# Attention with a top-8 MLP: candidates of fifteen token tiles picked early, the last tile run through the MLP whole

## The chip, the cores and the metric

One core of one Trainium2 chip runs the program. The metric is the device time of one execution in microseconds (us); several runs of a kernel are compared by their median.

## What is computed

The input is 2048 tokens of 448 values in bf16. Attention comes first: layer norm, 16 query heads of 28 values, one key and one value head for all of them, softmax, the output projection, and the residual sum h. Then comes an MLP for eight tokens only:

```python
x = layernorm(h)                         # 2048 x 448
r = x @ w_r                              # one score per token
idx = argsort(-r)[:8]
g = silu(x[idx] @ w_gate); u = x[idx] @ w_up      # 448 -> 1792
y = ((g * u) @ w_down) * sigmoid(r[idx])          # 1792 -> 448
out = h + x, and on the eight rows idx + y
```

So 2040 output rows are h + x, and eight rows get an addend. Which eight is known only when all 2048 scores are.

## The kernel before

Tokens are in 16 tiles of 128 (`NT`), which are also the 16 query blocks (`NB`). The attention loop runs over the blocks. In each, TensorE (PE) makes score tiles in groups of two or three PSUM banks, ScalarE (ACT) takes their exponential (L719), VectorE (DVE) makes a share of the exponentials by integer arithmetic (L744, L753, with GpSimd, POOL, in L755), and PE multiplies by V into the accumulator bank. A group is a unit of the loop; a block has 17. Units 2, 5 and 11 of a block (`TWO`) are two banks wide and not three, and the bank that is left over serves the odd jobs of other blocks (`misc`).

When a block's accumulator is complete, `close_acc` (L763) copies it to `Ot` and `post_block` (L599) divides by the softmax sum. It sends the sums through DRAM (`scr`) into a spread layout `Lc`, takes a reciprocal (L603), sends that back to DRAM, reads it broadcast over partitions into `Rb` (256 KB), and POOL multiplies (L609) into `On`: four DMAs on the queue of SyncE (SP), one after the other. `out_proj` (L612) is the projection of a block: four matmuls, the residual sum into `hbuf` (L617), the layer norm's statistics, `outf` = h + x (L644; L637 for the last tile), `xn` = x (L647; L640), and the tile's scores `r_col` (L650, L653). Blocks up to 13 have their `out_proj` two blocks later in the loop; block 14's is at the end of the last block, and block 15's behind the loop.

The tail comes behind the last `out_proj`, from L859 on. It checks that the softmax sums lie in a safe range and writes `flag`; every engine reads `flag` at its end, and an exact second program runs if it isn't zero. Then: the 2048 scores in one row by a DMA, the eight largest and their places (L885, L886), sums of bf16 parts that carry the indices through PE, one-hot matrices `oh` and `ohT`, 64 matmuls that gather the eight rows of x (L916), gate and up (56 matmuls each, eight columns wide), silu by exp and reciprocal, down (14 matmuls), and then for all 16 tiles a matmul with `ohT` that spreads the eight results over 128 rows, a sum with `outf` on ACT (L949) or DVE (L952), and four output DMAs of four tiles each.

Who runs what in which order is planned when the program is built: each operation is given to a graph with an engine, a duration, a priority and what it reads and writes; the planner (`plan`, L146) simulates the engines with these durations and fixes one order for each engine, which then runs it in order with semaphore waits. A lower priority number goes first. `G.prio` is mostly the time in the loop (64 units a block). DMAs all go through SP's order; the planner lets one land 2.7 us after its issue. Line L422 is the helper of every matmul, L425 of every transpose, L439 of every DMA.

Of the kernel before, what the change touches and what calls it, by code (L numbers as in the profile page):

```python
# [8 lines left out]
ALU = mybir.AluOpType  # L9
# [309 lines left out]
def _main(nc, G, sb, ps, psb, flag, scr, A_x, A_wq, A_wk, A_wv, A_wo, B_w_r, B_w_gate, B_w_up, B_w_down, out,  # L319
# [59 lines left out]
    ofin = xnT[:, :, :].rearrange("p a b -> p (a b)")[:, 0:NT * D].rearrange("p (t d) -> p t d", d=D)  # L379
# [113 lines left out]
    for i in range(4):  # L493
# [105 lines left out]
    def post_block(b):  # L599
# [56 lines left out]

    NVB = [0] + [4] * (NB - 1)
    LEAD = 4
    TWO = (2, 5, 11)
    LAG = 4  # L660
    slots = []
    for b in range(NB):
# [148 lines left out]
    else:  # L811
# [22 lines left out]
        for b in range(NB):  # L834
            at(64.0 * b + 64.0 + (LAG + 1.2) * m0, close_acc, b)
# [211 lines left out]
```

## Time and profile before

| | us |
|---|---|
| median of 3 runs (458.55 to 459.06) | 458.83 |
| the profiled execution's own time | 457.83 |
| its span, first to last instruction | 455.6 |
| last accumulator copy of the loop (L764) starts | 397.47 |
| last `out_proj` starts | 409.53 |
| eight largest scores: search starts | 417.28 |
| gather of eight rows starts | 425.04 |
| output stage starts | 441.78 |

The profile gives each instruction with its start from the beginning of the span, its length, the engine and the line. PE is the matmuls, PEld the weight loads. A bracket behind a row is the idle time of that engine before it and what ended it. PEclk is the granted clock of PE as a share of 2.4 GHz: 1.00 is the upper level, 0.50 the lower, 1.2 GHz. The loop takes 23.03 us a block.

### The profile page before, as it was taken

How to read it: one execution, taken by the hardware profiler on the slowest of the kernel's cores; microseconds unless marked ns; L12 is line 12 of the kernel's file. 1: busy time of each engine (PE TensorE's matmuls, PEld its weight loads, DVE VectorE, ACT ScalarE, POOL GpSimd, SP SyncE). 2: the span in 40 equal slices, each digit the busy share in tenths (PEclk: the TensorE clock that was granted, in tenths of full speed). 3: DMA queues.
4: the chain of work that ended last, by engine and by line, in shares of the span. 5: the costliest groups of instructions: out<-in, count | busy, mean ns of one | idle time of the engine just before them, and what ended most of it. 6: DMA issues, size and time to landing. Idle time of an engine off the chain costs nothing.

```text
span 455.6 us, 8732 instructions
## 1 busy us (share of the span) xinstructions
PE 335.5 (74%) x3583; PEld 121.5 (27%) x3583; DVE 343.5 (75%) x696; ACT 370.3 (81%) x309; POOL 188.6 (41%) x198
## 2 busy tenths in 40 slices
PE   3898787878787878787777777778787777601685
PEld 2454222212222323222222222222222122100630
DVE  6875668889797979797979797878787878626333
ACT  3778889999999999999999999898989898801012
POOL 3242134543636363636363636363636453740000
PEclk9999999999999999999999999999999999955565
DMA  7971000000000000000000000000000000000005
GB/s 211 230 205 28 2 12 15 9 19 27 1 27 0 22 6 24 3 24 4 22 7 17 10 16 12 11 15 12 16 10 19 4 23 6 23 25 1 1 1 167
DMA packets 15973, 14.68 MB, mean 32 GB/s; under 512 B 5992, under 2 KB 12920, under 8 KB 15928
## 3 DMA queue, kind: packets, MB, share of 16 engines
q1 hardware_dynamic: 15928, 14.05, 11.0%
q8 instruction: 31, 0.51, 0.5%
q14 instruction: 14, 0.11, 0.1%
HBM read 11.94 MB, written 2.10 MB: 31 GB/s over the span
## 4 chain that ended last, share of the span: by engine, by line
DVE 49%; PE 32%; ACT 10%; issue 5%; POOL 1%; DMA 1%; POOLq 0%; SPq 0%
PE ps L422 30%; DVE Y L744 24%; ACT P L719 10%; DVE Y L753 8%; DVE bn L619 2%; DVE junk L650 2%; DVE Q L527 2%; DVE Ot L764 2%; DVE hbuf L617 2%; DVE r_col L653 2%; PE ps L425 1%; DVE xnT L572 1%; DVE K L582 1%; DMA wq_sb<-in_A_wq_dram 1%; DVE idx L886 1%
## 5 line engine op out<-in xcount | busy, mean ns | idle before, releaser
L719 ACT ACTIVATE P<-ps 128x1536 bf16<-128x1536 f32 (+2 forms) x281 | 358.3, 1401 | 29.1 <-PE ps L422 26.7
L744 DVE TENSOR_SCALAR Y<-ps 128x512 int16<-128x512 f32 x240 | 165.3, 689 | 58.6 <-PE ps L422 58.5
L755 POOL TENSOR_TENSOR Y<-Y,step 128x1024 int32<-128x1024 int32 x60 | 113.5, 1892 | 151.3 <-DVE Y L753 89.7
L422 PE MATMUL ps<-Q,K 32*128 32x512 bf16 x1024 | 112.9, 388 | 61.1 <-DVE Y L744 45.6
L422 PE MATMUL ps<-Y,Vs 128*32 128x512 bf16 x960 | 88.2, 388 | 17.7 <-DVE Ot L764 11.3
L753 DVE TENSOR_SCALAR Y<-Y 128x2048 int16<-128x2048 int16 x120 | 82.6, 688 | 0.1
L422 PE MATMUL ps<-P,Vs 128*32 128x512 bf16 x784 | 75.7, 389 | 0.5 <-ACT P L719 0.5
L422 PEld LDWEIGHTS ps<-Q,K 32*128 32x128 bf16 x1024 | 33.3, 91 | 159.0 <-ACT P L719 126.3
L422 PEld LDWEIGHTS ps<-Y,Vs 128*32 128x32 bf16 x960 | 22.5, 94 | 60.9 <-issue 19.7
L422 PE MATMUL ps<-zero 128*32 128x512 bf16 x107 | 32.8, 386 | 0.0
L422 PEld LDWEIGHTS ps<-P,Vs 128*32 128x32 bf16 x784 | 19.0, 93 | 33.1 <-issue 29.9
L644 POOL TENSOR_SCALAR x_sb<-hbuf,st 128x448 bf16<-128x448 f32 x15 | 14.8, 984 | 31.4 <-DVE st L633 31.4
L609 POOL TENSOR_TENSOR On<-Ot,Rb 128x256 bf16<-128x256 f32 x32 | 23.4, 751 | 7.3 <-DMA Rb<-l_scr 7.3
L422 PE MATMUL ps<-xnT,wq_pad 112*128 112x128 bf16 x256 | 20.6, 229 | 0.6 <-DVE mv L540 0.6
L422 PE MATMUL ps<-wo_pad,On 128*128 128x448 bf16 x64 | 15.8, 369 | 6.5 <-POOL On L609 6.5
L595 POOL TENSOR_SCALAR Vs<-Vf 128x64 bf16<-128x64 f32 (+1 forms) x36 | 9.0, 249 | 22.7 <-DVE Vf L592 21.0
L617 DVE TENSOR_TENSOR hbuf<-ps,x_sb 128x448 f32<-128x448 f32 x16 | 9.9, 617 | 10.1 <-PE ps L422 10.1
L422 PEld LDWEIGHTS ps<-xnT,wq_pad 112*128 112x128 bf16 x256 | 15.5, 102 | 7.2 <-issue 7.1
L949 ACT ACTIVATE xnT<-ps 128x448 bf16<-128x448 f32 x8 | 4.4, 544 | 12.8 <-PE ps L422 12.8
L527 DVE TENSOR_SCALAR Q<-ps,qone 128x512 bf16<-128x512 f32 x16 | 11.9, 744 | 1.9 <-PE ps L422 1.9
L624 ACT ACTIVATE st<-st 128x1 f32<-128x1 f32 x1 | 0.2, 202 | 16.0 <-DVE st L621 16.0
L422 PEld LDWEIGHTS ps<-zero 128*32 128x32 bf16 x107 | 10.2, 97 | 7.0 <-issue 1.0
(124 smaller groups left out, 221.1 us busy)
## 6 DMA issues: line engine op xcount, KB each, us to landing
Rb<-l_scr SPq DMA_DIRECT2D x16, 256.0 KB
out_dram<-xnT SPq DMA_DIRECT2D x4, 448.0 KB, 3.4
wg_sb<-in_B_w_gate_dram SPq DMA_DIRECT2D x1, 1568.0 KB, 15.3
wu_sb<-in_B_w_up_dram SPq DMA_DIRECT2D x1, 1568.0 KB, 22.4
wd_sb<-in_B_w_down_dram SPq DMA_DIRECT2D x1, 1568.0 KB, 25.5
x_sb<-in_A_x_dram SPq DMA_DIRECT2D x3, 448.0 KB, 5.9
wq_sb<-in_A_wq_dram SPq DMA_DIRECT2D x2, 196.0 KB, 3.2
wo_pad<-in_A_wo_dram SPq DMA_DIRECT2D x4, 98.0 KB
```

What stands on the lines that cost most here:

```text
L422: return lambda e: e.matmul(o, lhsT=l, rhs=r, start=start, stop=stop)
L527: G.op(DV, lambda e: e.tensor_scalar(Q[:, q, :, :].rearrange("p g n -> p (g n)"), ps[:, bank, :], qone[:, 0:1], None, ALU.add), dvt(512), ...
L609: G.op(PO, lambda e, c=c: e.tensor_tensor(On[:, rb, c], Ot[:, rb, c], Rb[:, rb, c], ALU.mult), 750, reads=[("Ot", rb), ("Rb", rb)], writes ...
L617: G.op(DV, lambda e: e.tensor_tensor(hbuf[:, hr, :], ps[:, bank, 0:D], x_sb[:, t, :], ALU.add), dvt(D), reads=[pk(bank), ("x", t)], writes ...
L619: G.op(DV, lambda e: e.bn_stats(bn6[:, t, :], hbuf[:, hr, :]), dvt(D), reads=[("h", hr)], writes=[("bn6", t)])
L644: G.op(PO, lambda e: e.tensor_scalar(outf[:, t, :], hbuf[:, hr, :], st[:, t, 5:6], st[:, t, 6:7], ALU.mult, ALU.add), 800, reads=[("h", hr ...
L650: G.op(DV, lambda e: e.scalar_tensor_tensor(junk[:, :], hbuf[:, hr, :], st[:, t, 4:5], w_rb[:, :], ALU.mult, ALU.mult, accum_out=st[:, t, ...
L653: G.op(DV, lambda e: e.scalar_tensor_tensor(r_col[:, t:t + 1], st[:, t, 6:7], sw[:, 0:1], st[:, t, 2:3], ALU.mult, ALU.add), 80, reads=[(" ...
L719: G.op(AC, lambda e: e.activation(P[:, s0:s0 + w, :], ps[:, b0:b0 + w, :], ACT.Exp, bias=-(ZERO + SHIFT) * OCT, scale=OCT), w * 427 + 50, ...
L744: G.op(DV, lambda e: e.tensor_scalar(Y[:, y, 0, q, :].bitcast(I16), ps[:, VB, :], 0.0, 32639.0 - STEP[3], ALU.max, ALU.min), dvt(512), rea ...
L753: done = [G.op(DV, lambda e, c=c: e.tensor_single_scalar(y[c].bitcast(I16), y[0].bitcast(I16), STEP[c], ALU.add), 600, reads=r, writes=[(" ...
L755: G.op(PO, lambda e: e.tensor_tensor(y[3].bitcast(I32), y[0].bitcast(I32), step3[:, 0:1].broadcast_to([128, 1024]), ALU.add), 2050, reads= ...
```

## The change

The softmax division of blocks 14 and 15 no longer waits for DRAM: a matmul with a constant 0/1 matrix `selb` (fp32) spreads the sums over partitions in PSUM, ACT makes 1/L as exp(-ln L), and for block 15 DVE multiplies instead of POOL. (The sums still go to DRAM and into `Lc` for the check.) `out_proj` of block 14 moves from the end of the loop to unit 11 of the last block; in that block units 2, 7 and 11 are the narrow ones. Output tiles 0 to 14 are written as soon as `outf` is there, one DMA each, 112 KB.

A new `stage1` takes the eight best of tiles 0 to 14: the scores as 15 rows, `max` and `max_index` in each row, two small DMAs that put the 120 candidate scores in one row and their indices in one column, `max` and `max_index` over 120, fp32 matmuls that carry values and indices to columns and rows, the one-hot `oh`, 60 gather matmuls, 15 matmuls that gather the eight rows of `outf` (`os8`), gate, up, silu (ACT's own function) and down for these eight.

The last tile's 128 tokens all go through the MLP: transpose, gate and up with 128 columns (56 matmuls each, N = 128), silu, down (14 matmuls, N = 448). Whether a token is among the best eight is decided by counts: how many scores of its tile and how many of the candidates beat it (DVE, `wst`); the result is a factor of 0 or sigmoid(r). The candidates are tested in the same way against the last tile. Tile 15 is written with one DMA, and the eight candidate rows by an indirect DMA that POOL issues, behind all the other output DMAs. ACT loads the table with silu once, behind its last exp. The planner gets a priority of -3000 for the last tile's work; `stage1` has about 1015 to 1020, `out_proj` of block 15 1044.

The diff, cut to its core:

```diff
     def post_block(b, bank=None):
...
+        if b < NB - 2:
             G.op(DV, lambda e: e.reciprocal(Rc[:, rb, :], Lc[:, b, :]), 150, reads=[("Lc", b)], ...
             dma(scr[b, 1]..., Rc[:, rb, :], [("scr1", b)], reads=[("Rc", rb)])
             dma(Rb[:, rb, :], scr[b, 1]..., reads=[("scr1", b)]).lat = 3900.0
+        else:
+            G.op(PE, mm(ps[:, bank, :], selb[:, :], Ot[:, rb, :], True, True), 900, mode="F",
+                 reads=["selb", ("Ot", rb)], writes=[pk(bank)], prio=G.prio - 40)
+            G.op(AC, lambda e: e.activation(Rb[:, rb, :], ps[:, bank, :], ACT.Ln), 480, ..., prio=G.prio - 300)
+            G.op(AC, lambda e: e.activation(Rb[:, rb, :], Rb[:, rb, :], ACT.Exp, scale=-1.0), 520, ..., prio=G.prio - 300)
...
+                G.op(DV, lambda e, c=c: e.tensor_tensor(On[:, rb, c], Ot[:, rb, c], Rb[:, rb, c], ALU.mult), 335, ...
     def out_proj(b, bank):
...
+        if not tail:
+            evs.append(dma(out_v[:, t, :], outf[:, t, :], [("out", t)], reads=[("outf", t)], prio=G.prio + 30))
+    def stage1():
+        q = G.prio
+        G.op(DV, ... rp <- r_col ...); G.op(PE, ... rp x ident -> VB ...); G.op(DV, ... r16 ...)
+        G.op(DV, lambda e: e.max(c8[:, :], r16[:, :]), 200, ...)
+        dma(crow[0:1, :].rearrange("o (t k) -> o t k", k=8), c8[:, :], ["crow"], reads=["c8"])
+        G.op(DV, lambda e: e.max_index(i8[:, :], c8[:, :], r16[:, :]), 260, ...)
...
+        dma(cidx[:, :], i8f[:, :], ["cidx"], reads=["i8f"])
+        G.op(DV, lambda e: e.max(top8[:, :], crow[:, :]), 190, ...)
+        G.op(DV, lambda e: e.max_index(pos8[:, :], top8[:, :], crow[:, :]), 260, ...)
...
+        G.prio = q + 6
+        pieces([mm(psg[0:CK, ch, :], xn[:, t, ch * CK:(ch + 1) * CK], oh[:, t, :], t == 0, t == NT1 - 1)
+                for ch in range(NCH) for t in range(NT1)], 10, 35, ..., writes=[pk(VB)])
+        pieces([mm(ps[0:8, VB, 0:D], oh[:, t, :], outf[:, t, :], t == 0, t == NT1 - 1) for t in range(NT1)], 3, 189, ...
+        G.op(DV, lambda e: e.tensor_copy(os8, ps[0:8, VB, 0:D]), 540, ...)
+        pieces([mm(pt[:, fc, :], w_[0:CK, ch, fc * 128:(fc + 1) * 128], xselT[0:CK, ch, :], ch == 0, ch == NCH - 1)
+                for w_, pt in ((wg_sb, pg), (wu_sb, pu)) for fc in range(NFC) for ch in range(NCH)], 8, 30, ...
+        silu.append(G.op(AC, lambda e: e.activation(eg[:, :, :], pg[:, :, :], ACT.Silu), 260, ...))
+        G.op(DV, lambda e: e.tensor_tensor(guT[:, :, :], pu[:, :, :], eg[:, :, :], ALU.mult), 200, ...)
+        pieces([mm(ps[0:8, VB, 0:D], guT[:, fc, :], wd_sb[:, fc, :], fc == 0, fc == NFC - 1) for fc in range(NFC)], 3, 189, ...
...
-        at(64.0 * NB - 0.1, out_proj, NB - 2, VB)
-        at(64.0 * NB + (LAG + 1.3) * m0, out_proj, NB - 1, 0)
+                if b == NB - 1:
+                    at(64.0 * b + TWO[2] * m0 + 0.1, out_proj, b - 1, misc(b, TWO[2]))
+        at(64.0 * NB - 2.5 * m0, stage1)
+        at(64.0 * NB + (LAG + 1.3) * m0, out_proj, NB - 1, 4)
...
+    G.prio = hot
...
+    table = G.op(AC, lambda e: e.preload_act_table_set("silu_and_others"), 1300)
...
+    for bk, f0, f1 in where:
+        pieces([mm(gb[bk][:, f - f0, :], wg_sb[0:CK, ch, f * 128:(f + 1) * 128], xT[0:CK, ch, :], ch == 0,
+                   ch == NCH - 1) for f in range(f0, f1) for ch in range(NCH)], 8, 56, ...
+        silu.append(G.op(AC, ... e.activation(sil[:, f0:f1, :], gb[bk][:, 0:f1 - f0, :], ACT.Silu), ...
...
+    evs.append(dma(out_v[:, t, :], olast, [("out", t)], reads=["olast"]))
+    evs.append(G.op(PO, lambda e: e.indirect_dma_start(
+        out=out[0], out_offset=bass.IndirectOffsetOnAxis(ap=idxu[:, 0:1], axis=0), in_=rows8, in_offset=None,
+        bounds_check=S - 1, oob_is_err=False), 1000, reads=["rows8", "idxu"] + [("out", k) for k in range(NT1)],
+        writes=["scatter"], dma=True))
...
-    for t in range(NT):
...
-        fns = [mm(ps[:, bk, 0:D], ohT[:, t * 128:(t + 1) * 128], yp[:, :], True, not on_act)]
...
-            evs.append(dma(out_v[:, t - 3:t + 1, :], ofin[:, t - 3:t + 1, :], [("out", t)],
```

The first argument after a function or a list is the planner's duration in ns; of a list in `pieces` it is for one matmul, behind the number of matmuls in a piece.

## Rows read from the trace of the kernel before

**Rows 1.** Busy us by stretch: PE, PEld, DVE, ACT, POOL; PEclk, DMA share, GB/s.
```profile
366.00:389.00 23.00, 17.30 (x198) 5.16 (x194) 18.96 (x35) 21.79 (x18) 10.80 (x10) 1.00 0.06 21
389.00:398.00 9.00, 6.27 (x62) 1.66 (x58) 6.12 (x11) 7.58 (x6) 6.40 (x8) 1.00 0.03 10
398.00:408.00 10.00, 0.19 (x2) 0.09 (x2) 3.10 (x14) 0.00 (x0) 4.81 (x4) 0.62 0.09 29
...
425.00:442.00 17.00, 14.87 (x191) 10.86 (x191) 2.69 (x7) 0.26 (x1) 0.00 (x0) 0.52 0.01 2
```

**Rows 2.** Timeline, loop end to last stage: start, us, engine, line, operation, count [idle].
```profile
397.47 0.69 DVE L764 COPY Ot<-ps 128x512 f32<-128x512 f32 x1 [0.32 <-PE ps L422]
...
403.16 0.55 SPq L439 DMA_DIRECT2D Rb<-l_scr  x1
...
408.07 1.41 POOL L609 TENSOR_TENSOR On<-Ot,Rb 128x256 bf16<-128x256 f32 x2 [5.26 <-DMA Rb<-l_scr]
...
409.53 1.67 PE L422 MATMUL ps<-wo_pad,On 128*128 128x448 bf16 x4 [6.46 <-POOL On L609]
...
411.24 0.62 DVE L617 TENSOR_TENSOR hbuf<-ps,x_sb 128x448 f32<-128x448 f32 x1 [7.80 <-PE ps L422]
...
413.69 0.76 ACT L637 ACTIVATE x_sb<-hbuf,st 128x448 bf16<-128x448 f32 x1 [0.29 <-DVE st L633]
...
414.30 0.22 DVE L653 SCALAR_TENSOR_TENSOR r_col<-st,sw 128x1 f32<-128x1 f32 x1
...
425.04 6.13 PE L422 MATMUL ps<-oh,xn 128*112 128x8 bf16 x64 [1.48 <-DVE oh L910]
...
431.55 1.63 PE L422 MATMUL ps<-xselT,wg_sb 112*128 112x8 bf16 x56 [0.37 <-DVE xselT L919]
...
435.69 5.38 PE L422 MATMUL ps<-wd_sb,guT 128*8 128x448 bf16 x14 [1.01 <-DVE guT L932]
...
442.47 0.54 ACT L949 ACTIVATE xnT<-ps 128x448 bf16<-128x448 f32 x1 [8.99 <-PE ps L422]
```

**Rows 3.** Windows of 1 us, PE alone: start:end, length, PE busy, PEclk, DMA, GB/s.
```profile
400.00:401.00 1.00, 0.00 (x0) 0.72 0.07 7
...
441.00:442.00 1.00, 0.29 (x2) 0.80 0.00 0
...
445.00:446.00 1.00, 1.00 (x4) 0.50 0.81 275
```

**Rows 4.** Timeline, two blocks of the loop.
```profile
333.23 0.84 PE L422 MATMUL ps<-xnT,wq_pad 112*128 112x128 bf16 x12
...
364.32 0.55 SPq L439 DMA_DIRECT2D Rb<-l_scr  x1
...
366.03 0.72 POOL L644 TENSOR_SCALAR x_sb<-hbuf,st 128x448 bf16<-128x448 f32 x1
...
369.45 1.41 POOL L609 TENSOR_TENSOR On<-Ot,Rb 128x256 bf16<-128x256 f32 x2 [2.00 <-DMA Rb<-l_scr]
...
375.41 0.93 PE L422 MATMUL ps<-wo_pad,On 128*128 128x448 bf16 x4
```

**Rows 5.** DMA issues: out<-in, queue, count, KB each, median us to landing.
```profile
x_sb<-in_A_x_dram SPq DMA_DIRECT2D x2, 112.0 KB, 2.6
...
P<-r SPq DMA_DIRECT2D x1, 8.0 KB, 1.9
```

**Rows 6.** Groups by line and form: form, count | busy us, mean ns of one | idle.
```profile
L422 PE MATMUL ps<-xnT,wq_pad 112*128 112x128 bf16 x256 | 20.6, 229 | 0.6 <-DVE mv L540 0.6
...
L422 PE MATMUL ps<-wo_pad,On 128*128 128x448 bf16 x64 | 15.8, 369 | 6.5 <-POOL On L609 6.5
...
L422 PE MATMUL ps<-wd_sb,guT 128*8 128x448 bf16 x14 | 5.4, 574 | 1.0 <-DVE guT L932 1.0
```

**Rows 7.** Timeline, the first 10 us.
```profile
0.72 1.28 ACT L435 ACT_TABLE_LOAD   x1 [0.72 <-PEq L1032]
...
7.70 1.86 PE L422 MATMUL ps<-xnT,wq_pad 112*128 112x128 bf16 x16 [0.61 <-DVE mv L540]
```

More of the change, by code (lines that the diff above doesn't have):

```diff
@@ L659, in _main @@
     TWO = (2, 5, 11)
+    TWO_LAST = (2, 7, 11)
     LAG = 4
@@ L857, in _main @@
                     o.deps[p.idx] = o.deps.get(p.idx, False) or p.eng != PE
-    G.prio = 5000
+    if exact:
+        stage1()
+    ally = [] if exact else [("Y", n, c, k) for n in range(NY) for c in range(4) for k in range(4)]
+    t = NT - 1
+    T0 = G.prio
+    hot = -3000.0
+    G.prio = hot
+    G.op(DV, lambda e: e.tensor_copy(rp[:, t:t + 1], r_col[:, t:t + 1]), 70, reads=[("r", t)], writes=["rpl"])
+    G.op(DV, lambda e: e.tensor_copy(wst[:, 0:1], rp[:, t:t + 1]), 70, reads=["rpl"], writes=["wc"])
@@ new lines, in _main @@
+    G.op(DV, lambda e: e.tensor_scalar(dg[:, :], ident[:, :], wst[:, 0:1], None, ALU.mult), 100,
+         reads=["wc", "ident"], writes=["dg"])
+    G.op(AC, lambda e: e.activation(wst[:, 1:2], r_col[:, t:t + 1], ACT.Exp, scale=-1.0), 200, reads=[("r", t)],
+         writes=["w1"])
+    table = G.op(AC, lambda e: e.preload_act_table_set("silu_and_others"), 1300)
+    for o in G.ops:
+        if o.eng == AC and o not in silu and o is not table:
+            table.deps[o.idx] = False
+    G.op(DV, lambda e: e.tensor_scalar(wst[:, 1:2], wst[:, 1:2], 1.0, None, ALU.add), 70, reads=["w1"], writes=["w1"],
+         prio=6000)
@@ new lines, in _main @@
+    for o in silu:
+        o.deps[table.idx] = False
+    for bk, ub, f0, f1 in ((0, 4, 0, 4), (1, 5, 4, 8), (2, 7, 8, 12), (3, 3, 12, 14)):
+        o0 = 2 if ub == 3 else 0
+        pieces([mm(gb[ub][:, o0 + f - f0, :], wu_sb[0:CK, ch, f * 128:(f + 1) * 128], xT[0:CK, ch, :], ch == 0,
+                   ch == NCH - 1) for f in range(f0, f1) for ch in range(NCH)], 8, 56,
+               reads=["wu_sb", "xT"], writes=[pk(ub)])
+        G.op(DV, lambda e, ub=ub, f0=f0, f1=f1, o0=o0: e.tensor_tensor(
+            gu[:, f0:f1, :], gb[ub][:, o0:o0 + f1 - f0, :], sil[:, f0:f1, :], ALU.mult), dvt((f1 - f0) * 128),
+            reads=[pk(ub), ("sil", bk)], writes=[("gu", bk)])
@@ new lines, in _main @@
+    for bk, f0, f1 in where:
+        pieces([mm(ps[:, 0, 0:D], gu[:, f, :], wd_sb[:, f, :], f == 0, f == NFC - 1) for f in range(f0, f1)], 4, 189,
+               reads=["wd_sb", ("gu", bk)], writes=[pk(0)])
+    G.prio = hot + 100
+    G.op(PE, mm(ps[:, 5, 0:128], onesb[:, :], dg[:, :], True, True), 60, mode="F", reads=["onesb", "dg"],
+         writes=[pk(5)])
+    stt = lambda o, i0, s_, i1, op0, acc: (lambda e: e.scalar_tensor_tensor(o, i0, s_, i1, op0, ALU.mult, accum_out=acc))
+    G.op(DV, stt(scr128[:, :], ps[:, 5, 0:128], wst[:, 0:1], onesb[:, :], ALU.is_gt, wst[:, 3:4]), 280,
+         reads=[pk(5), "wc", "onesb"], writes=["scr128", "k3"] + ally)
```

289 lines of the change are left out of this document (167 added, 122 removed).

## The prediction

> **What bounds it now.** I read the busy time by stretch first [rows 1]. In the loop ACT is the full engine, 21.79 us of 23; PE has 17.30 and stays at the upper clock. From 398 on no engine is full for long: PE works 0.19 us of the ten up to 408 and 14.87 of the 17 from 425, there at the lower clock. The tail is a chain, so I then read the timeline behind the loop [rows 2]. The copy of the last accumulator starts at 397.47; `Rb` is issued at 403.16, the multiply on POOL begins at 408.07 after a DMA wait of 5.26, the projection at 409.53. Then come the scores (r ends at 414.52), the search for the eight, and at 425.04 the gather: 6.13 + 2 x 1.63 + 5.38 of PE work at the lower clock with small steps between, a spreading stage from 441.8, and the last output lands at the span's end, 455.6. So 58 us of 455.6 lie behind the loop, and the change rebuilds them all. What sets the end after it has to be found by adding up one engine at a time; for PE the clock decides, so I read windows of 1 us [rows 3]: it begins to fall in 400 to 401, some 3 us after the loop's last matmul, and 425 to 441, with PE nearly always busy, stays low. It rises only in 441 to 442, after the 448-wide down matmuls that began at 435.69, and is low again by 445.
>
> **The loop.** Block 14's division now has two ACT steps of 128x512 in the last block. A 448-wide one from PSUM takes 0.54 [rows 2], so 0.62 each; ACT is full there, so I take 1.2 later for the loop's end. The fp32 matmul with `selb` isn't in the trace: four 448-wide bf16 matmuls take 0.93 [rows 4], so one fp32 is between one and four of them, 0.25 and 1.1; I take 0.9, near the upper end, because it is 512 wide and fp32. PE has room for it. `out_proj` 14 moves up by about nine units; its PE time, 0.93, is covered by PE's idle quarter, and were that cover gone it would cost that 0.93 once. The 15 early output DMAs are 112 KB each and stand on SP behind a wait for POOL's `outf`. Behind them in SP's order is the next block's accumulator DMA. In the block shown `Rb` is issued at 364.32, `outf` is ready at 366.75, `On` is done at 370.86 and the projection starts at 375.41 [rows 4]: 4.5 us of slack, so zero, as long as no such DMA gets ahead of the division's own. The POOL constants (about ten small operations early on) cost nothing: POOL is busy 10.8 of 23 and `selb` is needed 14 blocks later.
>
> **From the accumulator to the last tile's x.** Copy at 398.7, done 399.4; `selb` to 400.3; two ACT steps to 401.6; two 256-wide multiplies on DVE at about 0.36 (448 wide is 0.62) to 402.4. The projection began at 409.53 before, so 7.1 us earlier. From its end to x: `hbuf` to the ACT step 2.45, the step 0.76 [rows 2], thus 3.2.
>
> **The candidates.** r of tile 14 needs DVE, which is busy with the loop until about 393 to 395; I take 395.2. Then two matmuls, two rounds of `max` and index over 120 to 128 values, some ten small DVE steps (the r step is 0.22; I take 0.15 to 0.3), five fp32 products (0.8 together) and one DMA on the path at 1.9 [rows 5]: 6.5 us, so the one-hot is there at 401.7, just when the last projection is ready. From there PE has enough to do, and **its sum sets the end**.
>
> **PE's sum behind 401.7**, at the lower and the upper clock:
> - 60 gather matmuls at 6.13/64 = 0.096: 5.75; upper not shown, taken as half, 2.9.
> - last projection: 1.67; 0.93.
> - 15 matmuls for `os8`, 448 wide: 5.38 [rows 2] less 0.57 for the last one [rows 6], over 13, is 0.37 apart, 5.6; 0.93 less the last one's 0.37, over 3, is 0.19 apart, 2.8.
> - transposes: 0.5; 0.3.
> - gate and up, 112 with 128 columns: 16 took 1.86 at the start [rows 7], less 0.23 for the last [rows 6], 0.109 apart, 12.2; 12 took 0.84 in the loop [rows 4], 0.055 apart, 6.2. I put the first to the lower clock, since it is twice the second.
> - down of the tile: 14 at 0.37, 5.2; 2.7. Down of the eight: the same.
> - gate and up of the eight: 2 x 1.63 = 3.3; at best half, 1.65.
>
> All low: 39.4. All high: 20.2. I take the gather, the projection and `os8` at the low clock (13.0), because the clock has fallen by then and the gather's kind of matmul left it low from 425 on [rows 3], and the rest at the upper one (transposes 0.3, gate and up 6.2, both downs 5.4) but the eight's gate and up at the only price shown, 3.3: together 28.2. In this trace the clock rose behind 448-wide matmuls [rows 2, 3], and `os8` and the projection are of that kind. Idle time of PE where one bank is handed on: copy of the gather 0.3, last product before down 0.6, silu and product of the eight 0.8, together 1.7. The end of PE's work: 401.7 + 28.2 + 1.7 = 431.6.
>
> **What is hidden.** Of the rest, the copy `xT` (at most the 0.69 of a 512-wide one [rows 2]), four silus (0.6 each), four products, the counting and the outputs lie beside PE. The table for silu is 1.28 [rows 7], between the last exp at about 407 and the first gate bank at 409; were it late, the first silu alone waits. The Trainium skill ("ScalarE: Activation LUTs", What ACT_TABLE_LOAD costs) adds about 1.4 us of drain to it; the row at the start shows 1.28 alone, and by the page's sum the first silu would wait about 1 us, with PE not waiting for it.
>
> **The end.** Last step on DVE: 0.6 (as the 448-wide sum, 0.62 [rows 2]). Then the indirect DMA, which waits on POOL for 15 output DMAs already landed. Nearest rows are 1.9 for 8 KB and 2.6 for 112 KB [rows 5]; I take 2.6, the longer, since POOL makes it and its list of waits comes first; the other end is 10, since nothing here shows this kind of DMA. The Trainium skill ("DMA: Bandwidth & Descriptors", Anatomy of one DMA) gives such a path about 2.0 us fixed; by that the end would be 0.6 earlier, and no run here shows it. 431.6 + 0.6 + 2.6 = 434.8 as the span, against 455.6. With the 2.2 that lie around the span it is 437.0, against 457.83; the median of the runs is 1.0 above that execution, so **438**. The shorter output stage, the division, the search and the gather are all in this difference of 20.8.
>
> **Rivals.**
> - *The clock stays low.* The waits between the pieces keep PE from a long dense series. For it: PE's work from 425 left the clock low up to 441. Against it: 112 gate and up matmuls are wide and in one series. Then 401.7 + 39.4 + 1.7 + 3.2 = 446.0, or **449**. The Trainium skill ("TensorE: Matmul & The Clock Gate", Why this matters for your kernels) warns that pauses between bursts bring the low clock back; by that rule this rival holds, and the fall at 400 agrees.
> - *All of it at the upper clock*, since the candidates come before the clock falls: 401.7 + 20.2 + 1.7 + 3.2 = 426.8, or **430**. Against it stands the fall at 400.
> - *The early part isn't early.* `stage1` does not do what it says if r of tile 14 comes at 399.5, as it does now: DVE and POOL are full in the last block, the moved projection gains nothing, PE idles about 4.3 us more before and between, and the time is **442**.
> - *Slower than before: the new DMAs block SP's queue.* If the planner puts a tile's output ahead of the write of the reciprocals, that write waits for `outf` until 366.75 [rows 4]; adding 1.9 for it and the 5.1 from `Rb`'s issue to `On`, `On` starts at 373.8 and not 369.45. POOL's next batch for DVE's share is held 4.3 us in each of some 14 blocks, with slack for part of it. It decides above 1.5 us a block (20.8/14); at 2.2 it costs 31 us and gives **469**. Against it: the planner issues a DMA when it is ready, and the reciprocals are ready 5 us earlier.
>
> **How the numbers follow.** Forecast 0.57 (its own range 433 to 443: start of the candidates 1.5 either way, end DMA up to 5, down of the eight at the low clock +2.5); low clock 0.16; upper clock 0.12; not early 0.10; slower 0.03; and 0.02 that all this comes to nothing. The range 430 to 449 leaves out half of each clock case and the slow one, some 0.17 to 0.2. About 0.2% is what a measurement of this kernel tells from no change, 0.9 us; four cases are far beyond: faster 0.95, same 0.02, slower 0.03.
>
> **What would show it.** Right: the last projection at 402 to 405; PE busy over 85% from there to about 432; clock row low to about 410 and high for gate and up; the last work a `rows8` step and an indirect DMA. The moved projection near 389 with r of tile 14 before 396; loop blocks still 23.03 us. Wrong: a block longer than 23.1 (queue), gate and up near 12 us (clock), PE waiting for `oh` behind the last projection (not early), or more than 5 us from `rows8` to the end (scatter).

## The result, and the profile after

The changed kernel takes 440.36 us (median of 4 runs, 435.83 to 441.12), the kernel before 458.94 beside it: a ratio of 0.957, 95% interval 0.950 to 0.964. The profiled execution took 440.31, its span is 438.4. In the table of the experiments one execution of e4_div14 (444.37 us) is left out of its median, since it lies over 1.5% above the fastest one of that kernel.

Busy time by stretch of the changed kernel; columns as in [rows 1], PE, PEld, DVE, ACT, POOL, then PEclk:

```profile
401.00:404.50 3.50, 1.74 (x12) 0.58 (x4) 1.90 (x9) 1.22 (x3) 0.00 (x0) 1.00 0.03 3
404.50:433.40 28.90, 27.80 (x348) 20.51 (x348) 11.65 (x50) 5.67 (x12) 0.00 (x0) 0.82 0.03 7
```

From 404.5 to 433.4 PE is busy 27.80 of 28.90 us. In the kernel before the 58 us behind the loop were a chain in which every engine waited; now one engine is full for most of what is left of them. The timeline of that stretch (start, length, engine, line, operation, count, idle before it):

```profile
401.37 0.69 DVE L805 COPY Ot<-ps 128x512 f32<-128x512 f32 x1 [0.44 <-PE ps L436]
...
402.12 1.13 PE L436 MATMUL ps<-Ot,wq_sb 128*128 128x512 f32 x2 [0.80 <-DVE Ot L805]
...
405.45 0.98 PE L436 MATMUL ps<-wo_pad,On 128*128 128x448 bf16 x3
...
405.77 0.28 DVE L847 TENSOR_TENSOR oh<-iota_c,bc 128x120 bf16<-128x120 f32 x1
...
406.22 5.72 PE L436 MATMUL ps<-oh,xn 128*112 128x8 bf16 x60
...
411.81 0.53 PE L436 MATMUL ps<-wo_pad,On 128*128 128x448 bf16 x1
...
412.27 4.84 PE L436 MATMUL ps<-x_sb,oh 128*8 128x448 bf16 x15
...
414.83 0.76 ACT L675 ACTIVATE xn<-hbuf,st 128x448 bf16<-128x448 f32 x1 [0.29 <-DVE st L671]
...
417.05 0.43 PE L439 MATMUL ps<-ident,xn 128*112 128x128 bf16 x4
...
418.15 1.28 ACT L978 ACT_TABLE_LOAD   x1
...
418.28 3.30 PE L436 MATMUL ps<-Y,wg_sb 112*128 112x128 bf16 x56
...
419.44 0.60 ACT L997 ACTIVATE Y<-ps 128x512 f32<-128x512 f32 x1
...
421.42 3.29 PE L436 MATMUL ps<-Y,wu_sb 112*128 112x128 bf16 x56
...
424.55 2.81 PE L436 MATMUL ps<-wd_sb,Y 128*128 128x448 bf16 x14
...
427.25 1.15 PE L436 MATMUL ps<-xselT,wg_sb 112*128 112x8 bf16 x40
...
428.26 1.54 PE L436 MATMUL ps<-xselT,wu_sb 112*128 112x8 bf16 x56
...
430.53 2.81 PE L436 MATMUL ps<-wd_sb,Y 128*8 128x448 bf16 x14 [0.61 <-DVE Y L868]
...
433.38 0.67 DVE L1035 SCALAR_TENSOR_TENSOR Y<-ps,wst,Y 8x448 bf16<-8x448 f32 x1 [2.90 <-PE ps L436]
...
435.11 1.12 POOL L1041 DMA_INDIRECT out_dram<-Y,idxu  x1 [35.67 <-issue]
```

The projection's fourth matmul stands behind the gather (411.81), so the last tile's x comes at 414.83 only; PE has the `os8` matmuls to do until then. The clock in windows of 1 us:

```profile
405.00:406.00 1.00, 1.00 (x11) 0.90 0.01 1
406.00:407.00 1.00, 1.00 (x11) 0.50 0.00 0
...
416.00:417.00 1.00, 1.00 (x6) 0.98 0.00 0
```

It falls at 405.9, behind the sparse stretch 401 to 404.5 (PE busy 1.74 of 3.50), stays at the lower level through the gather and nearly all of `os8`, and comes back behind the latter's 448-wide matmuls.

**Where the 17.2 us of span come from.** From the last accumulator copy to the end it was 58.13 us (397.47 to 455.6) [rows 2] and is 37.03 (401.37 to 438.4): 21.1 won. The last block, from copy to copy, took 19.81 and takes 22.04: 2.2 given back. The copy before it starts at 379.33 and not 377.66:

```profile
377.66 0.68 DVE L764 COPY Ot<-ps 128x512 f32<-128x512 f32 x1
```

```profile
379.33 0.68 DVE L805 COPY Ot<-ps 128x512 f32<-128x512 f32 x1
```

These 1.7 us are not the change's: e6_noos8, whose work is the same up to there, has this copy at 377.64 (last section). 21.1 - 2.2 - 1.7 = 17.2. How the 21.1 divide between the early candidates, the whole last tile and the output stage that is gone is not shown: no run takes out one of these alone. Because of the 1.7 the experiments are compared from the last accumulator copy on, beside their times. The blocks in between take 23.03 as before, so the fifteen early output DMAs cost the loop nothing.

### The profile page after: what moved, and what is told of

It is laid out like the page before. It is cut to its first block, busy times and chain, and to the rows that moved or that the text cites. A ratio compares the mean times of both kernels' runs of the same rounds, so it can differ in the third digit from the quotient of the medians.

```text
span 438.4 us, 9042 instructions
## 1 busy us (share of the span) xinstructions
PE 343.5 (78%) x3718; PEld 131.1 (30%) x3718; DVE 337.7 (77%) x708; ACT 371.7 (85%) x311; POOL 186.1 (42%) x200
## 4 chain that ended last, share of the span: by engine, by line
DVE 46%; PE 34%; ACT 13%; issue 4%; DMA 1%; POOL 0%; SPq 0%; POOLq 0%
PE ps L436 33%; DVE Y L785 24%; ACT P L760 13%; DVE Y L794 8%; DVE Ot L805 2%; DVE Q L549 2%; PE ps L439 2%; DVE junk L690 2%; DVE bn L657 2%; DVE hbuf L655 2%; DVE r_col L693 2%; DMA wq_sb<-in_A_wq_dram 1%; DVE xnT L594 1%; DVE K L604 1%; DVE Y L1016 0%
## 5 line engine op out<-in xcount | busy, mean ns | idle before, releaser
L785 DVE TENSOR_SCALAR Y<-ps 128x512 int16<-128x512 f32 x240 | 165.1, 688 | 58.2 <-PE ps L436 58.1
L436 PE MATMUL ps<-Y,Vs 128*32 128x512 bf16 x960 | 86.8, 385 | 16.6 <-DVE Ot L805 11.3
L436 PE MATMUL ps<-zero 128*32 128x512 bf16 x115 | 34.9, 386 | 0.0
L682 POOL TENSOR_SCALAR x_sb<-hbuf,st 128x448 bf16<-128x448 f32 x15 | 15.1, 1005 | 33.5 <-DVE st L671 33.5
L436 PEld LDWEIGHTS ps<-P,Vs 128*32 128x32 bf16 x784 | 18.9, 93 | 33.5 <-issue 30.1
L641 POOL TENSOR_TENSOR On<-Ot,Rb 128x256 bf16<-128x256 f32 x30 | 21.2, 724 | 1.5 <-DMA Rb<-l_scr 1.5
L1041 POOL DMA_INDIRECT out_dram<-Y,idxu x1 | 1.1, 1116 | 35.7 <-issue 35.7
L439 PE MATMUL ps<-ident,xn 128*112 128x128 bf16 x68 | 8.5, 291 | 6.3 <-DVE xn L572 6.3
L690 DVE SCALAR_TENSOR_TENSOR junk<-hbuf,st,w_rb 128x448 f32<-128x448 f32 x16 | 11.7, 733 | 0.0
```

Source lines behind the costliest of these rows:

```text
L436: return lambda e: e.matmul(o, lhsT=l, rhs=r, start=start, stop=stop)
L439: return lambda e: e.transpose(o, i, ident[0:p, 0:p])
L641: G.op(PO, lambda e, c=c: e.tensor_tensor(On[:, rb, c], Ot[:, rb, c], Rb[:, rb, c], ALU.mult), 750, reads=[("Ot", rb), ("Rb", rb)], writes ...
L682: G.op(PO, lambda e: e.tensor_scalar(outf[:, t, :], hbuf[:, hr, :], st[:, t, 5:6], st[:, t, 6:7], ALU.mult, ALU.add), 800, reads=[("h", hr ...
L690: G.op(DV, lambda e: e.scalar_tensor_tensor(junk[:, :], hbuf[:, hr, :], st[:, t, 4:5], w_rb[:, :], ALU.mult, ALU.mult, accum_out=st[:, t, ...
L785: G.op(DV, lambda e: e.tensor_scalar(Y[:, y, 0, q, :].bitcast(I16), ps[:, VB, :], 0.0, 32639.0 - STEP[3], ALU.max, ALU.min), dvt(512), rea ...
```

## The experiments

In the table "to rows8" is the time from the last accumulator copy to the start of the last step on the eight rows, "to end" to the end of the span, "block" the last block from copy to copy. The changed kernel has 32.0, 37.0 and 22.04.

| run | time, us | ratio to before, 95% | block | to rows8 | to end |
|---|---|---|---|---|---|
| e2_first | 440.26 | 0.954 to 0.963 | 22.03 | 32.5 | 37.6 |
| e3_warm | 440.04 | 0.954 to 0.964 | 22.03 | 32.5 | 37.3 |
| e6_noos8 | 436.56 | 0.944 to 0.958 | 22.03 | 30.4 | 36.3 |
| e4_div14 | 440.94 | 0.949 to 0.969 | 22.34 | 36.0 | 40.8 |
| e5_div15 | 445.70 | 0.964 to 0.979 | 22.03 | 38.5 | 44.4 |
| e7_plain | 437.09 | 0.947 to 0.963 | 22.04 | 31.9 | 36.1 |
| e8_late14 | 442.93 | 0.960 to 0.976 | 20.02 | 37.4 | 42.5 |
| e9_wide | 438.19 | 0.945 to 0.962 | 22.04 | 31.5 | 37.3 |
| e10_chain | 437.33 | 0.949 to 0.964 | 22.04 | 29.2 | 34.1 |
| e11_fold | 433.76 | 0.940 to 0.957 | 22.04 | 24.0 | 32.3 |
| e12_queue | 439.90 | 0.949 to 0.959 | 22.03 | 32.3 | 37.4 |
| e13_fold2 | 430.68 | 0.933 to 0.943 | 22.03 | 23.3 | 31.6 |

Single executions of one kernel lie 2 to 7 us apart, so a median of four tells some 3 us, and the readings below rest on the columns on the right. Each of these is from one profiled execution. The block is 22.03 to 22.05 in every run that leaves it alone; from `rows8` to the end the same scatter takes 4.8 to 5.9, so "to end" tells nothing under 1 us. How far the tail of one kernel varies from one execution to the next was not measured.

**Does the last tile's chain set the end, or PE's sum?** e2_first puts the last projection ahead of the gather:

```diff
         tail = b == NB - 1
+        if tail and not exact:
+            G.prio = -2900.0
```

> The last block's projection and its chain get the highest priority: its fourth matmul, which stands behind the gather at 411.8 in the changed kernel, starts before 407, and the last tile's x is ready about 6 us earlier. Theory (the sum of TensorE's work behind 404.5 sets the end, 28.9 us with almost no idle): the order changes and the sum does not, so TensorE's work ends within 1 us of the 433.4 of the changed kernel and the time within 0.3% of its 440.4. Rival (the last tile's chain of waits sets the end): 4 to 6 us faster than the changed kernel.

32.5 to `rows8`: the order changed, the sum did not, as the sum's theory says. But the trace shows that the chain was hardly shortened: x is ready 1.5 us earlier against the last copy, not the 6 that were expected. The row of the last tile's x (ACT) and what ran on DVE before it:

```profile
403.11 0.62 DVE L657 TENSOR_TENSOR hbuf<-ps,x_sb 128x448 f32<-128x448 f32 x1 [1.05 <-PE ps L436]
...
408.62 0.19 DVE L858 CAST xselT<-ps 112x32 bf16<-112x32 f32 x1 [3.24 <-PE ps L436]
...
408.98 0.15 DVE L671 TENSOR_SCALAR st<-st 128x1 f32<-128x1 f32 x1
...
409.23 0.76 ACT L677 ACTIVATE xn<-hbuf,st 128x448 bf16<-128x448 f32 x1 [3.77 <-DVE st L673]
```

`hbuf` starts at 403.11, but a step of the statistics stood in DVE's fixed order behind a copy that waits for the gather, so x came 6.1 us behind `hbuf`; in the changed kernel it is 2.45 (412.38 to 414.83). This was taken up again below.

**What is the low clock worth?** e3_warm puts twelve idle matmuls of 448 columns ahead of the tail, to keep the clock up; e6_noos8 leaves out 14 of the 15 matmuls of `os8` (the eight rows then lack most of h + x).

```diff
+        for k in range(12):
+            o = G.op(PE, mm(ps[:, 0, 0:D], wd_sb[:, k % NFC, 0:128], ...), ..., prio=G.prio + 100 + k, ...)
...
-        pieces([mm(ps[0:8, VB, 0:D], oh[:, t, :], outf[:, t, :], t == 0, t == NT1 - 1) for t in range(NT1)], ...
+        pieces([mm(ps[0:8, VB, 0:D], oh[:, t, :], outf[:, t, :], True, True) for t in range(1)], ...
```

> Twelve matmuls more, 448 wide, with no use for the result, in TensorE's gaps between the loop's end and the last projection (401 to 405). Theory: the clock no longer falls at 405.9, so the gather, the rest of the projection and the 448-wide gather of the eight rows (406.2 to 417.1, 10.9 us at the lower clock) take 6 to 8 us, and the time is 3 to 5 us below the changed kernel's 440.4. Rival A: the gather of 60 is held by its weight loads, not the clock, and stays at 5.7 us; then only the 448-wide ones gain, 2 to 2.5 us. Rival B: the clock falls all the same during the gather, and the added matmuls cost 0 to 1 us.

> Fourteen of the fifteen matmuls that gather the eight rows of h + x are left out (the eight output rows lack that part). They take 4.5 us at the lower clock in the changed kernel. Theory (TensorE's sum): 4 to 5 us faster than 440.4, less what the next matmuls lose if the clock then rises later (up to 3). Rival (the last tile's chain sets the end): its x is ready at 415.6 and its transposes wait for TensorE until 417.05, so no more than 1.5 us faster.

Windows of 1 us and one timeline row of e3_warm, then one row of e6_noos8:

```profile
404.00:405.00 1.00, 1.00 (x22) 0.96 0.00 0
405.00:406.00 1.00, 1.00 (x13) 0.50 0.06 16
...
426.00:427.00 1.00, 1.00 (x3) 0.50 0.35 115
```

```profile
425.99 4.19 PE L436 MATMUL ps<-wd_sb,Y 128*8 128x448 bf16 x14 [0.61 <-DVE Y L868]
```

```profile
415.91 5.59 PE L436 MATMUL ps<-Y,wg_sb 112*128 112x128 bf16 x56
```

In e3_warm the clock held until 405 and then fell in the middle of the gather, while PE was full (1.00 busy) with matmuls of 8 columns on 112 columns of weights. So the sparse stretch cannot be all that brings it down. The gather took 4.18 in place of 5.72, so the clock counts for it; but it fell a second time at 425 to 426, behind the small matmuls of the MLP of eight and a wait of 0.6, and the down product took 4.19 in place of 2.81. The changed kernel has the same series and the same wait, and its clock stays up there; why it fell here is not shown. Nothing was won: rival B held. In e6_noos8 4.3 us of wide matmuls are gone (4.84 to 0.54) and only 1.6 come back, because without them the clock is still low at gate, 5.59 for 3.30. What `os8` costs it pays back in part: with it the clock is up before gate starts, without it only at 420 to 421. The other limit is near as well: here the transposes start at 414.71, as soon as x is ready (414.66), as the rival says.

**What do the division and the projection of block 14 cost and earn?** e4_div14 takes block 14's division back to DRAM, e5_div15 block 15's; e8_late14 puts block 14's projection back to its old place in the plan, with the candidates' part behind it.

```diff
-        if b < NB - 2:
+        if b != NB - 1:            # e4_div14
+        if b != NB - 2:            # e5_div15
...
-                if b == NB - 1:
-                    at(64.0 * b + TWO[2] * m0 + 0.1, out_proj, b - 1, misc(b, TWO[2]))
...
-        at(64.0 * NB - 2.5 * m0, stage1)
+        at(64.0 * NB - 0.1, out_proj, NB - 2, VB)
+        at(64.0 * NB - 0.05, stage1)
```

> The softmax division of block 14 goes through DRAM again as in the kernel before; block 15's and all the rest stay. Theory: the two steps on ScalarE in the last block cost the loop 1.0 us and TensorE's wait for this block's division another 0.5 to 1, so the loop's last copy (401.4) is 1 to 2 us earlier; the candidates come 1 to 2 us later for their projection, TensorE waits for them a little, and the time is between 1 us below and 1 us above 440.4. Rival (the early division is what makes the candidates early, and they hold TensorE): 2 to 5 us slower than the changed kernel.

The block stayed long (22.34) without the two ACT steps, so this theory fell. The run alone does not clear them, since its projection starts 2.0 us later in the block; e8_late14, which has them, does. Of the 4.0 us more to `rows8`, 3.1 are three groups of PE at the lower clock: in the profiled execution the matmul with `selb` took 2.08 us and not 1.13 (PEclk 0.50), `os8` 5.46 and not 4.84, the eight's down product 4.38 and not 2.81. The rest goes with scores of tile 14 that are ready 1.9 us ahead of the last copy and not 2.7, as the rival says; the times (440.94 against 440.36) do not tell the two apart.

> Undoes one part alone: the projection of block 14 goes back to where it was before, at the end of the last block, with the candidates' part behind it; block 14's division stays new. The last block took 22.04 us against 19.81 in the kernel before, of which two ScalarE steps explain 1.0. Theory (the projection inside the last block costs the other 1.2 us): the last block falls to 20.6 to 21.0 us; what the tail gives back is the wait of the gather on the later scores, so that from the last accumulator copy to rows8 it is 32.0 plus 1 to 4 us, and the time 440 to 443. Rival (the projection in the block is free, the lengthening is something else): the last block stays at 21.8 to 22.1, the tail still grows by 1 to 4 us, 441.5 to 444.5.

The block fell to 20.02, 0.2 above the kernel before, with the two ACT steps in it; so the division's new form costs 0.2 there and the projection's new place 2.0. The tail grew by 5.4, not by 1 to 4. The timeline shows more than was expected. Last block of the changed kernel, then of e8_late14:

```profile
393.02 0.36 PE L436 MATMUL ps<-wo_pad,On 128*128 128x448 bf16 x1 [0.43 <-POOL On L641]
...
393.97 1.45 ACT L760 ACTIVATE P<-ps 128x1536 bf16<-128x1536 f32 x1 [0.49 <-PE ps L436]
...
395.91 2.79 ACT L760 ACTIVATE P<-ps 128x1536 bf16<-128x1536 f32 x2 [0.49 <-PE ps L436]
...
398.16 0.55 DVE L693 SCALAR_TENSOR_TENSOR r_col<-st,sw 128x1 f32<-128x1 f32 x1
...
399.20 1.45 ACT L760 ACTIVATE P<-ps 128x1536 bf16<-128x1536 f32 x1 [0.49 <-PE ps L436]
```

```profile
384.68 10.47 ACT L760 ACTIVATE P<-ps 128x1536 bf16<-128x1536 f32 x8
...
389.47 0.93 PE L436 MATMUL ps<-wo_pad,On 128*128 128x448 bf16 x4
...
396.26 0.21 DVE L693 SCALAR_TENSOR_TENSOR r_col<-st,sw 128x1 f32<-128x1 f32 x1
```

In both the projection starts at the same place, 13.7 and 13.8 us behind the copy before it, when `On` is ready. What differs is its bank: one of the six that the score groups use in turn, against `VB`. In the changed kernel ACT then stands 0.49 us before each of three exponentials; with `VB` eight run in one series of 10.47. ACT's idle time in the block is 22.04 - 18.88 = 3.16 against 20.02 - 18.56 = 1.46. That it is the bank is argued from these rows; a run with nothing but another bank was not made. The early place still pays: the step that makes the scores of tile 14 starts 3.2 us ahead of the last accumulator copy and not 0.6 behind it, and from the second last copy to `rows8` it is 54.1 us against 57.5.

> Undoes one part alone: block 15's softmax division goes by DRAM as in the kernel before, block 14's stays on TensorE and ScalarE. Theory (TensorE's sum behind the candidates sets the end): the last projection starts about 12 us after the last accumulator copy as before (409.53 - 397.47 = 12.1), not 4.1, but TensorE has the 60 gather and 15 row matmuls and the small MLP matmuls (2.7 us) to do meanwhile, so from the last accumulator copy to the start of rows8 it is 32.0 us plus 0 to 3 us, the time +0 to +3 us on 440.4. Rival (the quicker division is what the change earns, the last tile's chain sets the end): the 8 us by which the projection is later come back whole, 447 to 449 us.

The rival was nearer, though 445.7 is short of its 447: 6.5 us more to `rows8`, 5.3 more in time. Rows of e5_div15:

```profile
416.95 0.74 DVE L644 TENSOR_TENSOR On<-Ot,Rb 128x256 bf16<-128x256 f32 x2
...
419.97 1.65 PE L436 MATMUL ps<-wo_pad,On 128*128 128x448 bf16 x4
...
424.92 0.67 PE L439 MATMUL ps<-ident,xn 128*112 128x128 bf16 x4 [3.30 <-ACT xn L675]
```

The division does not come late alone; the multiply then stands in DVE's order behind the copy of `os8`, and the projection behind the whole MLP of eight. The projection is 14.8 us later (18.9 behind the copy, not 4.1); other work of PE covers 8.3 of them. Of the 6.5 that show, 4.9 are idle time of PE, 3.30 in one piece, and 1.6 are gate, 4.88 for 3.30, because the clock had fallen. So the sum of PE's work sets the end only as long as the last tile's chain runs beside it.

**What does the scatter cost?** e7_plain sends the eight rows with a plain DMA to rows 0 to 7; their places are left out.

```diff
-    evs.append(G.op(PO, lambda e: e.indirect_dma_start(...
+    evs.append(dma(out[0][0:8, :], rows8, ["scatter"], ...))
```

> The eight rows go out by one plain DMA of SyncE to rows 0 to 7 in place of the indirect DMA, so their places in the output are left out. It prices the scatter, which took 4.35 us from the end of rows8 to the end of the span. If the 1.06 us in which GpSimd stands before its DMA, and the DMA itself, belong to the indirect form, a plain one ends 2.2 to 3.2 us after rows8: 1.2 to 2.1 us less, a time of 438.3 to 439.2. If the wait on the fifteen output DMAs costs SyncE's queue the same, it is 0.5 us or less.

From `rows8` to the end 4.2 us in place of 5.0: 0.8 less, between the two expectations. The DMA itself gained more: SP's last wait ends 2.6 us behind the end of `rows8` and not 3.9. In e7_plain DVE's last record, a `DRAIN` at 434.7, comes 0.4 behind that wait, so the end is then no longer the DMA's alone. The scatter is thus worth 1.3 us to the landing and 0.8 to the end, in one execution each; with the scatter this stretch varies by 1.1 between the runs.

**The gather in another shape.** e9_wide has the one-hot as weights and the 448 columns of x moving, 15 matmuls, then a copy and four small transposes; e10_chain adds e2_first's priority and keeps the gather's copy, and two reductions that wait for DRAM, behind the last tile's steps on DVE; e12_queue has that order with the narrow gather.

```diff
-        pieces([mm(psg[0:CK, ch, :], xn[:, t, ch * CK:(ch + 1) * CK], oh[:, t, :], ...) for ch in range(NCH) for t in range(NT1)], ...
+        pieces([mm(ps[0:8, 0, 0:D], oh[:, t, :], xn[:, t, :], t == 0, t == NT1 - 1) for t in range(NT1)], 3, 189, ...
+        G.op(DV, lambda e: e.tensor_copy(xs8[:, :], ps[0:8, 0, 0:D]), 540, reads=[pk(0), ("st6", NT1)], ...
...
+    G.op(DV, lambda e: e.tensor_reduce(Lmm[:, 0:1], lall, AX.X, ALU.min), 330, reads=lk + [("r", NT1)], ...
+        G.op(PE, [tr(psb[0:CK, 1, ch * 8:ch * 8 + 8], xs8[:, ch * CK:(ch + 1) * CK], 8) for ch in range(NCH)], ...
```

> The gather of the eight rows in another shape: 15 matmuls with the one-hot as weights and 448 columns of the normalised tokens moving, a copy of 8x448 and four small transposes, in place of 60 matmuls of 8 columns that load 112 columns of weights each (5.72 us, at the lower clock). Nothing is left out. Theory A (the clock falls because of those 60 small matmuls, and the sum of TensorE's work sets the end): the gather takes 2.8 us and the fifteen row matmuls behind it 2.8 to 3.2 us at the upper clock in place of 5.72 + 4.84; less what the last tile's chain then shows, from the last accumulator copy to rows8 it is 27 to 29 us in place of 32.0, the time 435 to 437.5. Rival B (the clock falls in this stretch whatever the shape): 4.8 us each, 9.6 in place of 10.6, 439 to 440. Rival C (the last tile's chain sets the end): the gather is shorter and the time the same, TensorE idle ahead of the last tile's transposes.

> Both together, and the queue on VectorE mended: the gather in its wide shape, the four matmuls of the last projection in one piece ahead of it, and the last tile's normalisation ahead of the copy of the gathered rows and of the two reductions over Lc, which wait for a DMA round trip. Nothing is left out. Alone, the early projection moved the span from the last accumulator copy to rows8 from 32.0 to 32.55 us and the wide gather to 31.47. Theory (TensorE's work and the last tile's chain lie one beside the other with under 1 us between them, so that either alone gives nothing and both together give what they save): projection at +4.1, gather and rows 5.8 to 7.7, transposes and their copy 1.5, gate, up and down 9.4, the small MLP 2.7 + 0.6 + 2.8 and the broadcast 0.2: 28.4 to 30.0 us to rows8, a time of 436.8 to 438.4. Rival (the clock takes back whatever is saved, as in the run with dummy matmuls): 31 us or more, 439.5 or more.

> The run with the early projection and the mended VectorE queue, but with the gather in the narrow shape of the changed kernel (60 matmuls of 8 columns): it parts the queue from the shape in the run that joined both. Nothing is left out. Theory (the work of TensorE behind the projection fills the time to the last tile's transposes anyway: gather 5.7, then the rows, 4.4 to 5.4, transposes wherever they fall): from the last accumulator copy to rows8 31.5 to 32.6 us, as with the early projection alone (32.55), a time of 439.5 to 441; then the joined run's gain is the wide shape's, opened by the queue. Rival (the queue on VectorE was the loss, the shape nothing): 29 to 30.5 us, 436.5 to 438.5.

Rows of e9_wide, of e12_queue and of e10_chain:

```profile
406.32 4.68 PE L436 MATMUL ps<-xn,oh 128*8 128x448 bf16 x15
...
410.84 3.00 PE L436 MATMUL ps<-x_sb,oh 128*8 128x448 bf16 x15
...
414.07 0.36 PE L436 MATMUL ps<-wo_pad,On 128*128 128x448 bf16 x1
...
416.92 0.76 ACT L675 ACTIVATE xn<-hbuf,st 128x448 bf16<-128x448 f32 x1 [0.29 <-DVE st L671]
...
417.73 0.68 PE L439 MATMUL ps<-ident,xn 128*112 128x128 bf16 x4
...
418.93 5.43 PE L436 MATMUL ps<-Y,wg_sb 112*128 112x128 bf16 x56
```

```profile
407.00 5.72 PE L436 MATMUL ps<-oh,xn 128*112 128x8 bf16 x60
...
413.17 4.55 PE L436 MATMUL ps<-x_sb,oh 128*8 128x448 bf16 x15
```

```profile
406.83 4.07 PE L436 MATMUL ps<-xn,oh 128*8 128x448 bf16 x15
```

Alone, the wide shape gives 2.9 us on PE (7.7 for gather and `os8` in place of 10.6) and 0.5 to `rows8`: the projection's last matmul is behind both again, the last tile's x is late, and its transposes start as soon as x is there (417.68, 417.73). PE fills the time with the small MLP, the clock falls, gate takes 5.43. Alone, the order gives nothing (32.3). Both together give 2.8 (29.2): the size that theory A gave, and rival C as the reason why it was not to be had alone. The medians say 437.3 against 440.4; the ratio's interval covers the changed kernel's, so this gain is read from the traces. PE's work and the tile's own chain reach the last tile's transposes at nearly the same time: in the changed kernel x is ready at 415.59, and PE comes to them at 417.05.

**A version that beats both.** On top of e10_chain, e11_fold lets the eight rows ride as columns 128 to 135 behind the last tile's in gate and up, puts their down product ahead of the tile's, and lets POOL see the fifteen output DMAs early; e13_fold2 moves the small transposes ahead of `os8` besides.

```diff
-    xT = big[:, 5376:5888].rearrange("p (c n) -> p c n", n=128)
+    xT = big[:, 5712:6256].rearrange("p (c n) -> p c n", n=136)
...
+    G.op(PO, lambda e: e.memset(nhalf[:, 0:1], -0.5), 100, reads=[("out", k) for k in range(NT1)], writes=["nhalf", "seen"], prio=3000)
...
-             mode="F", reads=["xs8", "ident"], writes=[pk(1)], prio=G.prio - 25)
+             mode="F", reads=["xs8", "ident"], writes=[pk(1)], prio=-3300.0)      # e13_fold2
```

> A version meant to beat both kernels. On top of the run before: the eight picked rows ride as eight more columns behind the last tile's 128 through gate and up (56 + 56 matmuls of 136 columns in place of 112 of 128 and 112 of 8), their down part stands ahead of the last tile's, and GpSimd waits for the fifteen output DMAs early, by a memset of its own, ahead of the scatter. Nothing is left out. Theory (TensorE's sum plus the DMA that ends last): 2.7 + 0.6 us less than the run before on TensorE, 0.4 more for the eight columns; the end is the last tile's plain DMA, some 3.5 us behind the last copy, in place of the scatter's 4.35; from the last accumulator copy to the end 30 to 32.5 us in place of 37.0, a time of 433.4 to 436. Rival (gate and up must now wait for the picked rows, whose chain of copy, transposes and copy is then what ends last; or the clock falls for it): 34 us or more, 437.4 or more.

> The folded version with the small transposes of the picked rows ahead of the fifteen row matmuls, and the copy of these rows behind the two copies that gate waits for. In the folded run TensorE stood 1.17 us ahead of gate, for these copies. Nothing is left out. Theory (they now lie beside the row matmuls): gate starts 0.8 to 1.2 us earlier, from the last accumulator copy to the end 31.0 to 31.6 us in place of 32.27, a time of 432.5 to 433.2. Rival (TensorE now stands ahead of the transposes for as long, or the clock falls in that gap): 32.0 us or more, 433.6 or more.

433.8 and 430.7 us. The last, at a ratio of 0.938 (0.933 to 0.943), lies below the changed kernel's whole interval; its gate starts 0.7 earlier than e11_fold's (0.8 to 1.2 expected), and it ends 31.6 us behind the last copy as against 32.3, just at the edge of what was expected. Its time is 1.8 us below the expected range, because the last copy of this execution starts at 396.99 and e11_fold's at 399.43, which the edit does not touch. Its end:

```profile
420.28 0.67 DVE L1037 SCALAR_TENSOR_TENSOR Y<-ps,wst,Y 8x448 bf16<-8x448 f32 x1 [1.55 <-PE ps L433]
422.01 1.11 POOL L1045 DMA_INDIRECT out_dram<-Y,idxu  x1 [25.76 <-issue]
...
423.75 0.34 SPq L450 DMA_DIRECT2D out_dram<-Y  x1
```

## Why the prediction held, and where its steps were off

The forecast was 438.0 with 430 to 449, the time is 440.4: the case that was named likeliest came about. The span is 3.6 us longer than the forecast 434.8, and that is three errors, one of them the other way. The time is only 2.4 longer, because what lies between span and median was taken as 3.2 and is 1.9. So the mechanism held, and that the number came so near is in part luck: the errors that lengthen the span sum to 6.2 us.

- **The one-hot came at 406.05, not 401.7** (+4.35). Of this 2.7 is the loop's end, at 401.37 for 398.7: 1.7 from the start of the execution, and 1.0 because the last block is 2.2 longer and not 1.2. The step that failed is "`out_proj` 14 moves up ... covered by PE's idle quarter": PE's time was covered, but the bank that it takes was not looked at, and the block is 2.0 longer (e8_late14; that the bank is the reason is argued, not shown). The two ACT steps, for which 1.2 was taken, cost 0.2. The other 1.7 is that the one-hot is ready 4.7 us behind the last copy and not 3.0. Half of it is the scores of tile 14, ready 2.7 us ahead of the loop's end (398.71) and not 3.5; half is the chain from them to the one-hot, 7.3 us and not 6.5: its exp stands in ACT's order behind the logarithm of block 15's division, and PE waits 1.00 us for what comes of it.
- **Two signs of being right did not come.** The projection of block 14 was to be near 389 and its scores ready before 396; it starts at 393.02, and they are ready at 398.71, of which 1.7 is the start of the execution. In the full loop the new division of block 14 has `On` 13.6 us behind the accumulator copy, the old one had it after 15.1; the matmul with `selb` starts only 5.5 us behind the copy, and POOL's multiply 3.0 behind the end of the exp. So the projection moves up by two units (2.7 us) and not by about nine.
- **PE's sum was right** (-2.6). Gather 5.72 (5.75 forecast), projection 1.51 (1.67), `os8` 4.84 (5.6), transposes 0.43 (0.3), gate and up 6.59 (6.2), the eight's gate and up 0.54 + 1.15 + 1.54 = 3.23 (3.3), both downs 5.62 (5.4): 27.9 against 28.2. From the one-hot to the last product's end it is 27.3 and not 29.9: idle time is 1.0 and not 1.7, the projection had begun 0.6 before the one-hot was ready, and the groups, each timed to its last end, overlap by 1.0. The clock did what was assumed, low for gather, most of the projection and `os8`, high from the transposes on. (The price of the eight's gate and up was a row at the lower clock, and it came true at PEclk 1.00: 1.54 for 56 matmuls.)
- **The end took 5.0 us and not 3.2** from `rows8` on (+1.9). POOL's DMA starts 1.06 us behind `rows8`, which had no term, and lands 2.8 after its issue (2.6 forecast); the span ends 0.5 behind the landing. This is just over the 5 us that the prediction gave as a sign of being wrong. That POOL's list of waits comes first, as the step says, is not the reason: with these waits done 25 us before, in e13_fold2, it is still 1.06.

4.35 - 2.6 + 1.9 = 3.6. The early part was early, so this rival did not come about; the low clock held for 10 us, and the rest ran at the upper level, as weighed; the queue of SP was never late, and the blocks in the loop are 23.03. The Trainium skill ("TensorE: Matmul & The Clock Gate", Why this matters for your kernels) puts such a fall down to pauses between bursts of matmuls. That does not account for the falls here: ahead of the one at 405.9 the longest pause of PE is 1.27 us, and in e3_warm the clock fell in a series without a pause. The drain behind a table load, on another page of the Trainium skill ("ScalarE: Activation LUTs", What ACT_TABLE_LOAD costs), did not show: the load ends at 419.43 and the first silu starts at 419.44.

What the prediction missed in kind is how near its own rival was: the last tile's chain is as long as PE's sum, so the statement that the sum sets the end is true for this order only (e5_div15, e9_wide, e10_chain).

## What to carry to other kernels

Where a full engine and a chain of short steps reach the same point at nearly the same time, shortening one alone gains little (0.5 us by the wide gather, nothing by the order, 2.8 by both); an edit that gives nothing there is to be tried once more together with one on the other side before it is dropped. A job that is moved into a tuned loop can cost by the buffers it takes out of the rotation (argued above from rows), and not only by its time on an engine. For a gather by a one-hot matrix, have the one-hot as weights and the wide rows moving: 15 matmuls, a copy and four small transposes do what 60 matmuls did, and in e9_wide and e10_chain the clock, low at their start, came back during them (409 to 410), where with the 60 it stayed low until 416.

## What was not expected of the hardware

- The fp32 matmul 128x128 with 512 columns stands as two rows of PE and took 1.13 us at the upper clock, just above the bound of 1.1 that was taken, and 2.08 at the lower (e4_div14).
- Most of the spread between the profiled executions is made in the first 40 us, where their order of work is the same: the first accumulator copy lies 4.9 us apart, the second last 4.7. There is one profile of each kernel, so that this holds between executions of one kernel is argued. The same eight transposes in the changed kernel and in e3_warm:

```profile
29.16 1.10 PE L439 MATMUL ps<-ident,xn 128*112 128x128 bf16 x8
```

```profile
27.18 0.65 PE L439 MATMUL ps<-ident,xn 128*112 128x128 bf16 x8
```

  Where they take 1.10 (the changed kernel, e5_div15, e9_wide, e10_chain, e12_queue), PE's matmuls have the lower clock's spacing up to about 37 us and the first accumulator copy starts at 58.2 to 58.5; where they take 0.65, at 53.6 to 55.5 (the kernel before and the other eight), and e3_warm has the quicker spacing from 23 us on. PEclk shows 1.00 in both all that time, so here the lengths say more than that row. What decides it is open.
- In e11_fold and e13_fold2 the last output DMA has landed 3.1 us before the span ends, and no engine shows work in between. The reading of `flag` is not it: in e13_fold2 all engines have read it by 424.7, and SP's waits for the output DMAs are over by 425.7. The last records ahead of the end at 428.6 are a `DRAIN` of ACT at 427.6, of PE at 428.2 and of DVE at 428.3; what they wait for is not shown.
